# Values as the weights of their product, agents streamed twice, and more load buffers in an agent-attention and cosine-FFN kernel

## The chip, the cores and the metric

The kernel runs on one core of a Trainium2 chip. The metric is the device time in microseconds of one execution; lower is better. Inputs lie in device memory in the layouts that the kernel asks for (q and k transposed, v in tiles of 120 rows, the weights as 64-bit patterns), and the output is written transposed.

The core has five engines that matter here. PE multiplies matrices: it loads up to 128 columns of weights (recorded as LDWEIGHTS, row PEld), then streams the other operand past them (MATMUL, row PE) and writes to PSUM, an accumulator memory of eight banks with 512 float32 columns each. DVE and ACT work element by element and read PSUM. POOL works on SBUF, the main on-chip memory. SP issues the DMA transfers between device memory and SBUF, in order.

## The reference

Cut to what matters, with B = 4 batches, N = 12480 tokens each, C = 128 channels, 49 agents and a hidden width of 2048:

```python
def sm(a, b):                              # softmax over b's rows of a @ b.T / sqrt(128)
    s = scale * (a @ b.transpose(0, 2, 1)); s = s - s.max(-1, keepdims=True)
    e = np.exp(s)
    return e / (e.sum(-1, keepdims=True) + 1e-09)
agent_v = sm(agents, k) @ v                # 49 x 128 per batch
attn    = sm(q, agents) @ agent_v          # N x 128 per batch
h       = attn.reshape(B * N, 128) @ w_in  # 49920 x 2048
out     = (h * np.cos(h)) @ w_out          # 49920 x 128
```

The tokens of k and v meet only in `agent_v`. A batch's tokens of q cannot pass through the second half before its `agent_v` is there.

## The kernel before, in words

**Tiles.** A batch's 12480 tokens are 13 groups (`NG`) of 960 (`GRP`); a group is 8 tiles (`GT`) of 120 tokens (`TT`). A load of a group of q, k or v is 480 KB.

**One batch's agents** (class `Agents`, with `Fast` on top of it). `scores` (L144) loads a group of k into one of three `xt` buffers and makes eight products with 120 columns of k as the weights and the 49 agents streaming (helper `scores`, L81, the product at L87). They land in one PSUM bank; ACT copies them to `s` (L153), and DVE keeps a running maximum (L157). `top`, `across` and `spread` reduce the maximum over the tiles and partitions and lay it out over all partitions. `shift` subtracts it (DVE or POOL, L182), `exp` takes the exponential on ACT, `add` sums them on POOL. `values` (L195) loads a group of v into one of three `vt` buffers and makes eight products with the exponentials of a tile (120 x 49) as the weights and v (120 x 128) streaming (L200). The result, 49 x 128, is added by DVE to `o` (L204). `total` and `turn` follow: `turn` (L213) multiplies `o` by `fold`, a 49 x 113 matrix made of two identities. That transposes `o` and puts it side by side twice, in columns 0 to 48 and 64 to 112, as `av` (L219). It also forms the inverse of the sums. `project` multiplies `av` with `w_in`, so the hidden layer of batch b is then one product of 113 rows per token.

**The weights.** `w_in` and `w_out` arrive as float64 and are turned into float32 on DVE by eight bit operations for each chunk of 512 columns (L103 to L111). The raw chunk stands in a `vt` buffer, as the groups of v do. `product` forms w_in times w_out, for which the transposes are at L129 and the products at L133.

**The steps.** From the 832 steps (L469) comes the output. Each takes 480 tokens and 256 hidden columns: two products into a two-bank PSUM tile `ph` (L476; three such tiles), the cosine on ACT (L479, into one of three `c` buffers), (cos - 1) times h on DVE (L481), and four steps later two products into the output (L497). There are 208 steps per batch.

**What sets the order.** Before the steps, batch 0's agents, the weights and the first three groups of q are worked off alone, in the order of a list, `pre`: `pre(n, f, ...)` puts f at place n, and the places are run one after the other. Key scores of group g stand at place g, a chunk of `w_in` at 3c + 1, the first queries at 14, 15 and 16, shift, exponential and values of group k at 15 + k, 16 + k and 17 + k, a chunk of `w_out` at 16 + 3c and its product a place later, `turn` at 30. During the steps, a second list, `plan`, puts the agents of batches 1 to 3 and the queries of all groups between steps; `extra` gives each piece with products a step of its own. The framework may still move an engine's instructions past their neighbours when it lays out the queues (the exponentials of the steps and the load of the sine table are held in place with `keep_in_program_order`). On the chip the engines take their instructions from their queues in order; SP likewise, and a load waits there until its buffer is free.

**PSUM.** Six banks are the three `ph` tiles, two banks are the small tiles `one`. The key scores, the values, the queries and the transposes before the change all take `one`.

The lower part of the program, from L519, is a slower path for inputs out of range; it isn't run with these inputs.

Of the kernel before, what the change touches and what calls it, by code (L numbers as in the profile page):

```python
# [40 lines left out]
def agent_attention_cos_ffn(ctx, tc, qT, kT, v, agT, w_in, w_out, outT):  # L41
# [17 lines left out]

    ident = const.tile([P, P], F32, name="ident")  # L60
    make_identity(nc, ident)

    fold = const.tile([NA, KR], F32, name="fold")
    nc.gpsimd.memset(fold, 0.0)
    for part in (fold[:, :NA], fold[:, HI:]):
        nc.gpsimd.affine_select(out=part, in_=part, compare_op=ALU.not_equal, fill=1.0,
                                base=0, pattern=[[-1, NA]], channel_multiplier=1)
    ones = const.tile([P, 1], F32, name="ones")
    nc.gpsimd.memset(ones, 1.0)
    half_pi = const.tile([P, 1], F32, name="half_pi")  # L70
# [7 lines left out]

    fits = const.tile([KR, NB], F32, name="fits")

    def scores(sb, src, b, ps):  # L81

        xt = sb.tile([P, GRP], F32, name="xt", bufs=3)
        nc.sync.dma_start(xt, src)
        ps = ps[:TT, :GT * NA].rearrange("p (t a) -> p t a", a=NA)
        for t in range(GT):
            nc.tensor.matmul(ps[:, t, :], xt[:, t * TT:(t + 1) * TT], ag[:, b, :], start=True, stop=True)  # L87
        return ps

    class Weights:  # L90


        def __init__(self, sb, psum, tag, bufs):
            self.sb, self.psum = sb, psum
            self.scratch = dict(name=tag, bufs=bufs)

        def single(self, src, out):

            raw = self.sb.tile([P, 512, 2], U32, name="vt", bufs=3)
            nc.sync.dma_start(raw, src)  # L100
            lo, hi = raw[:, :, 0], raw[:, :, 1]
            ex, sign, man = (self.sb.tile([P, 512], U32, **self.scratch) for _ in range(3))
            nc.vector.tensor_scalar(ex, hi, 20, 0x7FF, op0=ALU.logical_shift_right, op1=ALU.bitwise_and)  # L103
            nc.vector.tensor_scalar(sign, hi, 0x80000000, None, op0=ALU.bitwise_and)
            nc.vector.tensor_scalar(ex, ex, 1151.0, 896.0, op0=ALU.min, op1=ALU.max)
            nc.vector.tensor_scalar(man, hi, 0xFFFFF, 0x100000, op0=ALU.bitwise_and, op1=ALU.bitwise_or)
            nc.vector.tensor_scalar(ex, ex, 896.0, None, op0=ALU.subtract)
            f = man.bitcast(F32)
            nc.vector.scalar_tensor_tensor(f, lo, 2.0 ** -32, man, op0=ALU.mult, op1=ALU.add)
            nc.vector.scalar_tensor_tensor(ex, ex, 23, sign, op0=ALU.logical_shift_left, op1=ALU.bitwise_or)  # L110
            nc.vector.scalar_tensor_tensor(out, f, 2.0 ** -20, ex.bitcast(F32), op0=ALU.mult, op1=ALU.mult)  # L111
# [25 lines left out]
    class Agents:  # L137

        def __init__(self, sb, psum, b, alone=False):
            self.sb, self.psum, self.b, self.alone = sb, psum, b, alone

        def scores(self, g):  # L144
            sb = self.sb
            if g == 0:
                self.s = sb.tile([TT, NT, NA], F32, name="s", bufs=1)
                self.run = sb.tile([TT, GT, NA], F32, name="run", bufs=1)
                self.o = sb.tile([NA, P], F32, name="o", bufs=2)
                self.es = sb.tile([TT, GT, NA], F32, name="es", bufs=1)  # L150
            ps = scores(sb, kT[self.b, :, g * GRP:(g + 1) * GRP], self.b, self.psum())
            s = self.part(g)
            nc.scalar.copy(s, ps)  # L153
            if g == 0:
                nc.vector.tensor_copy(self.run, s)
            else:
                nc.vector.tensor_max(self.run, self.run, s)  # L157

        def part(self, g, n=1):
            return self.s[:, g * GT:(g + n) * GT, :]  # L160
# [32 lines left out]
                nc.gpsimd.tensor_add(self.es, self.es, self.part(g))  # L193

        def values(self, g):  # L195
            vt = self.sb.tile([TT, GT, P], F32, name="vt", bufs=3)
            nc.sync.dma_start(vt, v[self.b, :, g * GT:(g + 1) * GT, :])
            e, po = self.part(g), self.psum()[:NA, :P]
            for t in range(GT):
                nc.tensor.matmul(po, e[:, t, :], vt[:, t, :], start=(t == 0), stop=(t == GT - 1))  # L200
            if g == 0:
                nc.vector.tensor_copy(self.o, po)
            else:
                nc.vector.tensor_add(self.o, self.o, po)  # L204

        def total(self):

# [2 lines left out]
            nc.vector.tensor_reduce(self.es2[:, :NA], self.es.rearrange("p t a -> p a t"), axis=AX.X, op=ALU.add)  # L210
            nc.vector.tensor_copy(self.es2[:, HI:], self.es2[:, :NA])

        def turn(self):  # L213

            pa = self.psum()
            nc.tensor.matmul(pa[:, :KR], self.o, fold, start=True, stop=True)
            nc.tensor.matmul(pa[:KR, 256:257], self.es2, ones[:TT], start=True, stop=True)
            self.av = self.sb.tile([P, KR], F32, name="av", bufs=1)
            nc.vector.tensor_copy(self.av, pa[:, :KR])  # L219
            z = self.sb.tile([KR, 1], F32, name="z", bufs=1)  # L220
            nc.vector.tensor_scalar_add(z, pa[:KR, 256:257], EPS)
            self.rz = self.sb.tile([KR, 1], F32, name="rz", bufs=1)
            nc.vector.reciprocal(self.rz, z)

# [2 lines left out]
    class Fast(Agents):  # L227

        def project(self, c, a):

            cs = slice(c * 512, (c + 1) * 512)
            pw = self.psum()
            nc.tensor.matmul(pw[:KR], self.av, win[:, cs], start=True, stop=True)  # L233
            if c == 0:
                self.big = self.sb.tile([KR, DFF // 512], F32, name="big", bufs=1)
            nc.scalar.activation(a[:, cs], pw[:KR], AF.Copy, scale=self.rz)
            x = a[:, cs].bitcast(F32)
            nc.vector.tensor_reduce(self.big[:, c:c + 1], x, axis=AX.X, op=ALU.max, apply_absolute_value=True)

            on = nc.vector if self.alone else nc.gpsimd  # L240
            on.tensor_scalar(a[:, cs], x, FAST_MAX, -FAST_MAX, op0=ALU.min, op1=ALU.max)

        def project_out(self, wio, b1, b2):
# [25 lines left out]
    with ExitStack() as pools:  # L269
# [76 lines left out]
            t = sb.tile([1, 1], F32, name="sine", bufs=1)  # L346
            tc.keep_in_program_order(nc.scalar.activation(t, half_pi[:1], AF.Sin))

        ab = [Fast(sb, small, b, b == 0) for b in range(NB)]
        if NG == 13:  # L350
            pieces0 = [(0, 1, 2), (3, 4, 5, 6, 7), (8, 9, 10, 11, 12)]
            pieces1 = [(0, 1, 2, 3), (4, 5, 6, 7), (8, 9, 10, 11, 12)]
# [6 lines left out]
        for g in range(NG):  # L359
            pre(g, ab[0].scores, g)  # L360
        for c in range(NF // 4):
            pre(3 * c + 1, ws.w_in, c)
        pre(NG, ab[0].top)
        pre(NG, ab[0].across)
        pre(NG, ab[0].spread)
        for i, n in enumerate(pieces[0][0]):
            pre(NG + 1 + i, query, n, pieces[0][0])
        for j, (g, n) in enumerate(lots):
            for k in range(g, g + n):
                pre(NG + 2 + k, ab[0].shift, k, 1, nc.gpsimd if k % 3 == 2 else nc.vector)  # L370
# [13 lines left out]
            ws.product(c, w_parts.pop(c), po_w[0], wio)  # L384

        for c in range(NF // 4):
            pre(NG + 3 + 3 * c, w_out_of, c)
            pre(NG + 4 + 3 * c, w_product, c)
        pre(end - 2, query_exp, pieces[0][0])
        pre(end - 1, query_sums, pieces[0][0])  # L390
        pre(end - 1, query_weights, 0)
        pre(end, sine_table)
        pre(end, query_turned, 0)
        pre(end, ab[0].total)
        pre(end, ab[0].turn)
        for c in range(DFF // 512):
            pre(end + 1, ab[0].project, c, a[0])
        pre(end + 1, ab[0].project_out, wio, b1[0], b2[0])
# [36 lines left out]
        for b in range(1, NB):  # L435
# [20 lines left out]
                plan(t, ab[b].add, g)  # L456
                t = extra(t, ab[b].values, g) + 1
            plan(t, ab[b].total)
            t = extra(t + 1, ab[b].turn) + 1
            i = b % 2  # L460
            for c in range(DFF // 512):
                t = extra(t, ab[b].project, c, a[i]) + 1
# [56 lines left out]
    with tc.If(far):  # L519
        with ExitStack() as pools:  # L520
# [72 lines left out]
                nc.sync.dma_start(dst, osb)  # L593

            for b in range(NB):
                ab = Agents(sb, small, b, True)
                for g in range(NG):
                    ab.scores(g)
                ab.top()
# [5 lines left out]
                    ab.add(g)  # L605
                    ab.values(g)
                ab.total()
                ab.turn()
                for c in range(DFF // 512):
                    cs = slice(c * 512, (c + 1) * 512)  # L610
                    pw = small()
# [32 lines left out]
```

## Time and profile before

| | |
|---|---|
| Median of 3 runs | 1332.18 us (1330.01 to 1332.27) |
| Profiled execution | 1332.36 us, span 1330.6 us |
| Before the steps | about 121 us of the span |
| PE, DVE, ACT, POOL busy | 1231.0, 1094.5, 1010.4, 331.2 us |
| Mean granted clock of PE | 0.978 |
| Moved by DMA | 107.74 MB |

A row of the profile names the line, the engine, the operation, the tile written and the tiles read, the shapes and the count, then the busy time in us with the mean of one in ns, then the idle time ahead of them and what ended it. A float32 product is recorded as two LDWEIGHTS and two MATMUL records; where the products of the steps read float32r, there is one of each. Matmuls are pipelined, so the mean of one is longer than the distance between two.

### The profile page before, as it was taken

To read this page: it belongs to the slowest core of one execution; us is meant where nothing else is said; L and a number is where in the kernel's file an instruction comes from. 1 tells how busy PE (TensorE), PEld (TensorE's weight loads), DVE (VectorE), ACT (ScalarE), POOL (GpSimd) and SP (SyncE) were. 2 spreads that over 40 slices of the span, in tenths; PEclk is the share of its full clock that TensorE was granted. 3 is DMA by queue.
4 is the path that set the end of the run, shared out by engine and by line. 5 is a ranking of instruction groups with operands and counts; after the bars stand their busy time and mean duration, and the time that the engine had idled before them with its cause. 6 is when DMAs were issued, how large, how long until landed. Compare 5 with 4: busy or idle time off the path is not lost.

```text
span 1330.6 us, 17227 instructions
## 1 busy us (share of the span) xinstructions
PE 1231.0 (93%) x6357; PEld 971.9 (73%) x6357; DVE 1094.5 (82%) x1221; ACT 1010.4 (76%) x1115; POOL 331.2 (25%) x357
## 2 busy tenths in 40 slices
PE   8878999999799999996999999996999999999997
PEld 8866778777587788775876688775786666666664
DVE  3566878878778988887789988887779999999997
ACT  1124778866768987667689988767679999999997
POOL 1231211331512122315122211514113222122220
PEclk9979989999899999998999999998999999999999
DMA  6665234233242132332420033230420000000000
GB/s 209 172 163 134 90 102 122 89 92 105 72 119 75 59 105 89 120 107 74 117 60 30 30 104 123 72 105 30 119 75 16 30 30 30 30 15 31 30 30 33
DMA packets 31017, 107.74 MB, mean 81 GB/s; under 512 B 3436, under 2 KB 3820, under 8 KB 30924
## 3 DMA queue, kind: packets, MB, share of 16 engines
q1 hardware_dynamic: 30924, 106.54, 26.6%
q8 instruction: 53, 0.87, 0.3%
q14 instruction: 40, 0.33, 0.1%
HBM read 80.97 MB, written 25.56 MB: 80 GB/s over the span
## 4 chain that ended last, share of the span: by engine, by line
PE 67%; DVE 13%; ACT 11%; issue 5%; POOL 2%; DMA 1%; ACTq 0%; SPq 0%; POOLq 0%
PE ph L476 23%; PE one L497 16%; PE one L87 14%; DVE r L481 10%; PE one L200 7%; ACT c L479 5%; ACT osb L499 3%; PE one L492 2%; PE one L333 2%; PE one L493 1%; DVE mx L304 1%; ACT e L314 1%; POOL es L193 1%; PE one L233 1%; ACT p L335 1%
## 5 line engine op out<-in xcount | busy, mean ns | idle before, releaser
L481 DVE SCALAR_TENSOR_TENSOR r<-c,ph 128x960 fp32r<-128x960 f32 x832 | 926.2, 1149 | 119.9 <-ACT c L479 109.6
L479 ACT ACTIVATE c<-ph,half_pi 128x960 f32<-128x960 f32 x832 | 864.4, 1066 | 208.4 <-PE ph L476 191.3
L476 PE MATMUL ph<-pT,a 113*128 113x480 f32 x1664 | 540.1, 406 | 24.2 <-DVE r L481 20.8
L497 PE MATMUL one<-r,w 128*128 128x480 f32 x1664 | 516.1, 390 | 0.7 <-DVE r L481 0.7
L476 PEld LDWEIGHTS ph<-pT,a 113*128 113x128 f32 x1664 | 287.3, 191 | 150.9 <-DVE r L481 88.3
L497 PEld LDWEIGHTS one<-r,w 128*128 128x128 f32 x1664 | 309.2, 190 | 52.0 <-issue 7.6
L87 PEld LDWEIGHTS one<-ag,xt 128*120 128x120 f32 x1664 | 216.9, 206 | 25.3 <-ACT osb L499 10.8
L324 POOL TENSOR_TENSOR p<-e,rz 120x392 f32<-120x392 f32 x52 | 43.9, 846 | 758.6 <-PE one L333 716.8
L87 PE MATMUL one<-ag,xt 128*120 128x49 f32 x1664 | 215.6, 285 | 8.7 <-DMA xt<-kT 5.0
L200 PE MATMUL one<-vt,s 120*49 120x128 f32 x832 | 112.7, 294 | 37.0 <-ACT osb L499 26.7
L200 PEld LDWEIGHTS one<-vt,s 120*49 120x49 f32 x832 | 97.9, 134 | 53.6 <-ACT osb L499 27.9
L339 POOL TENSOR_TENSOR pT<-p,pT 49x480 fp32r<-49x480 f32 x104 | 126.6, 1217 | 8.0
L338 POOL CAST pT<-p 49x480 fp32r<-49x480 f32 x104 | 60.8, 585 | 59.1 <-ACT p L335 54.1
L153 ACT COPY s<-one 120x392 f32<-120x392 f32 x52 | 25.2, 485 | 45.0 <-PE one L87 44.8
L499 ACT COPY osb<-one 128x480 f32<-128x480 f32 x104 | 57.8, 555 | 2.1 <-PE one L497 2.1
L304 DVE TENSOR_REDUCE mx<-one 120x8 f32<-120x392 f32 x52 | 29.3, 564 | 35.3 <-PE one L87 35.2
L492 PE MATMUL one<-pT,b 113*128 113x480 f32 x104 | 46.3, 445 | 11.7 <-ACT osb L499 6.7
L182 POOL TENSOR_TENSOR s<-s,mxb 120x1568 f32<-120x1568 f32 (+2 forms) x13 | 35.8, 2778 | 72.8 <-DVE mxb L178 72.8
L193 POOL TENSOR_TENSOR es<-es,s 120x392 f32<-120x392 f32 x48 | 50.0, 1042 | 13.1 <-ACT s L186 9.4
L492 PEld LDWEIGHTS one<-pT,b 113*128 113x128 f32 x104 | 19.7, 189 | 34.3 <-issue 12.5
L157 DVE TENSOR_TENSOR run<-run,s 120x392 f32<-120x392 f32 x48 | 27.0, 562 | 18.8 <-ACT s L153 18.8
L333 PE MATMUL one<-ident,p 120*113 120x120 f32 x208 | 37.9, 283 | 4.4 <-ACT s L153 1.8
(84 smaller groups left out, 405.1 us busy)
## 6 DMA issues: line engine op xcount, KB each, us to landing
xt<-kT SPq DMA_DIRECT2D x52, 480.0 KB, 3.5
xt<-qT SPq DMA_DIRECT2D x52, 480.0 KB, 3.5
vt<-v SPq DMA_DIRECT2D x52, 480.0 KB, 4.3
outT<-osb SPq DMA_DIRECT2D x51, 480.0 KB, 2.5
vt<-w_in SPq DMA_DIRECT2D x4, 512.0 KB, 4.7
vt<-w_out SPq DMA_DIRECT2D x4, 512.0 KB, 5.2
outT<-osb SPq DMA_DIRECT2D x2, 240.0 KB, 2.0
ag<-agT SPq DMA_DIRECT2D x1, 98.0 KB, 2.1
```

Source lines behind the costliest of these rows:

```text
L87: nc.tensor.matmul(ps[:, t, :], xt[:, t * TT:(t + 1) * TT], ag[:, b, :], start=True, stop=True)
L193: nc.gpsimd.tensor_add(self.es, self.es, self.part(g))
L200: nc.tensor.matmul(po, e[:, t, :], vt[:, t, :], start=(t == 0), stop=(t == GT - 1))
L333: nc.tensor.transpose(pt[:KR, t * TT:(t + 1) * TT], p_in[n % 2][:, t, :KR], ident[:TT, :TT])
L338: nc.gpsimd.tensor_copy(pT[own, c], p[own])
L339: nc.gpsimd.tensor_sub(pT[other, c], p[own], pT[own, c].bitcast(F32))
L476: nc.tensor.matmul(ph[:, j, :CH], ai[:, f], pTs[q % 3][:, c], start=True, stop=True)
L479: nc.scalar.activation(cos, h, AF.Sin, bias=half_pi, scale=1.0)
L481: nc.vector.scalar_tensor_tensor(r, cos, 1.0, h, op0=ALU.subtract, op1=ALU.mult)
L492: nc.tensor.matmul(po, b1[k], pTs[q % 3][:, c], start=True, stop=False)
L497: nc.tensor.matmul(po, w1[:, f, :], r[:, j, :], start=False, stop=(f == NF - 1))
L499: nc.scalar.copy(osb[:, c * CH:(c + 1) * CH], po)
```

## The change

The operands of the values' product change places: a tile of v (120 x 128) is now the weights, and the 49 exponentials stream, twice over, through an access pattern with a step of zero (`twice`). The result is 128 x (2 x 49). It is written to columns 0 to 48 and 64 to 112 of a bank (`copies`), which is the layout of `av`. So `o`, `fold` and the fold product go, and `turn` becomes `inverse`, with only the product for the sums.

Batch 0 gets `wide`, a function that hands out the steps' two-bank tiles `ph`. Its key scores stream the agents twice as well: four tiles of 98 columns in each of the two banks, of which ACT reads the first 49 of each 98. Its values accumulate over all 13 groups in one bank of one such tile, and DVE copies them out once at the end. In batches 1 to 3 each group's values still go to a small tile, and DVE adds them to `av`.

Batch 0's odd groups of k are loaded into the steps' `c` buffers, the even ones into `xt`. The raw chunks of the weights get two buffers of their own (`raw`), and `vt` has four. In the list `pre`, chunks of `w_in` move from 3c + 1 to 3c + 2, chunks of `w_out` and their products one place later, and the first three queries from 14, 15, 16 to 14, 18, 22.

```diff
-    fold = const.tile([NA, KR], F32, name="fold")
...
+    def twice(x):
+        return x.unsqueeze(1).to_broadcast([x.shape[0], 2, NA])
...
+    def scores_twice(xt, src, b, ps):
+        nc.sync.dma_start(xt, src)
+        ps = ps[:TT, :, :HT * 2 * NA].rearrange("p h (t x a) -> p h t x a", x=2, a=NA)
+        for t in range(GT):
+            nc.tensor.matmul(ps[:, t // HT, t % HT], xt[:, t * TT:(t + 1) * TT], twice(ag[:, b, :]),
+                             start=True, stop=True)
+        return ps[:, :, :, 0, :]
...
-            raw = self.sb.tile([P, 512, 2], U32, name="vt", bufs=3)
+            raw = self.sb.tile([P, 512, 2], U32, name="raw", bufs=2)
...
-                self.o = sb.tile([NA, P], F32, name="o", bufs=2)
+                av = sb.tile([P, 2 * HI], F32, name="av", bufs=2)
+                self.av, self.sums = av[:, :KR], self.copies(av)
+                nc.gpsimd.memset(av[:, NA:HI], 0.0)
...
-            ps = scores(sb, kT[self.b, :, g * GRP:(g + 1) * GRP], self.b, self.psum())
+            src = kT[self.b, :, g * GRP:(g + 1) * GRP]
             s = self.part(g)
-            nc.scalar.copy(s, ps)
+            if self.wide is None:
+                nc.scalar.copy(s, scores(sb, src, self.b, self.psum()))
+            else:
+                if g % 2:
+                    xt = sb.tile([P, 2, CH], F32, name="c", bufs=3).rearrange("p j x -> p (j x)")
+                else:
+                    xt = sb.tile([P, GRP], F32, name="xt", bufs=3)
+                ps = scores_twice(xt, src, self.b, self.wide())
+                nc.scalar.copy(s.rearrange("p (h t) a -> p h t a", h=2), ps)
...
+        def copies(self, x):
+            return x[:, :2 * HI].rearrange("p (x a) -> p x a", x=2)[:, :, :NA]
...
-            vt = self.sb.tile([TT, GT, P], F32, name="vt", bufs=3)
+            vt = self.sb.tile([TT, GT, P], F32, name="vt", bufs=4)
             nc.sync.dma_start(vt, v[self.b, :, g * GT:(g + 1) * GT, :])
-            e, po = self.part(g), self.psum()[:NA, :P]
+            lone = self.wide is not None
+            if g == 0 or not lone:
+                self.po = self.copies(self.wide()[:, 0] if lone else self.psum())
+            e, po = self.part(g), self.po
             for t in range(GT):
-                nc.tensor.matmul(po, e[:, t, :], vt[:, t, :], start=(t == 0), stop=(t == GT - 1))
-            if g == 0:
-                nc.vector.tensor_copy(self.o, po)
-            else:
-                nc.vector.tensor_add(self.o, self.o, po)
+                nc.tensor.matmul(po, vt[:, t, :], twice(e[:, t, :]), start=(t == 0 and (g == 0 or not lone)),
+                                 stop=(t == GT - 1 and (g == NG - 1 or not lone)))
+            if g == (NG - 1 if lone else 0):
+                nc.vector.tensor_copy(self.sums, po)
+            elif not lone:
+                nc.vector.tensor_add(self.sums, self.sums, po)
...
-        def turn(self):
+        def inverse(self):
             pa = self.psum()
-            nc.tensor.matmul(pa[:, :KR], self.o, fold, start=True, stop=True)
-            nc.tensor.matmul(pa[:KR, 256:257], self.es2, ones[:TT], start=True, stop=True)
-            self.av = self.sb.tile([P, KR], F32, name="av", bufs=1)
-            nc.vector.tensor_copy(self.av, pa[:, :KR])
+            nc.tensor.matmul(pa[:KR, :1], self.es2, ones[:TT], start=True, stop=True)
...
-        ab = [Fast(sb, small, b, b == 0) for b in range(NB)]
+        def pair():
+            return ps_h.tile([P, 2, 512], F32, name="ph")
+        ab = [Fast(sb, small, b, None if b else pair) for b in range(NB)]
...
-            pre(3 * c + 1, ws.w_in, c)
+            pre(3 * c + 2, ws.w_in, c)
...
-            pre(NG + 1 + i, query, n, pieces[0][0])
+            pre(NG + 1 + 4 * i, query, n, pieces[0][0])
...
-            pre(NG + 3 + 3 * c, w_out_of, c)
-            pre(NG + 4 + 3 * c, w_product, c)
+            pre(NG + 4 + 3 * c, w_out_of, c)
+            pre(NG + 5 + 3 * c, w_product, c)
```

More of the change, by code (lines that the diff above doesn't have):

```diff
@@ L61, in agent_attention_cos_ffn @@
     make_identity(nc, ident)
-    fold = const.tile([NA, KR], F32, name="fold")
[L64 to L67, printed above, removed]
     ones = const.tile([P, 1], F32, name="ones")
@@ L137, in agent_attention_cos_ffn, with __init__ @@
     class Agents:
-        def __init__(self, sb, psum, b, alone=False):
-            self.sb, self.psum, self.b, self.alone = sb, psum, b, alone
+        def __init__(self, sb, psum, b, wide=None):
+            self.sb, self.psum, self.b, self.wide = sb, psum, b, wide
         def scores(self, g):
@@ L211, in total @@
             nc.vector.tensor_copy(self.es2[:, HI:], self.es2[:, :NA])
-        def turn(self):
+        def inverse(self):
             pa = self.psum()
-            nc.tensor.matmul(pa[:, :KR], self.o, fold, start=True, stop=True)
-            nc.tensor.matmul(pa[:KR, 256:257], self.es2, ones[:TT], start=True, stop=True)
-            self.av = self.sb.tile([P, KR], F32, name="av", bufs=1)
-            nc.vector.tensor_copy(self.av, pa[:, :KR])
+            nc.tensor.matmul(pa[:KR, :1], self.es2, ones[:TT], start=True, stop=True)
             z = self.sb.tile([KR, 1], F32, name="z", bufs=1)
-            nc.vector.tensor_scalar_add(z, pa[:KR, 256:257], EPS)
+            nc.vector.tensor_scalar_add(z, pa[:KR, :1], EPS)
             self.rz = self.sb.tile([KR, 1], F32, name="rz", bufs=1)
@@ L238, in project @@
             nc.vector.tensor_reduce(self.big[:, c:c + 1], x, axis=AX.X, op=ALU.max, apply_absolute_value=True)
-            on = nc.vector if self.alone else nc.gpsimd
+            on = nc.vector if self.wide else nc.gpsimd
             on.tensor_scalar(a[:, cs], x, FAST_MAX, -FAST_MAX, op0=ALU.min, op1=ALU.max)
@@ L394, in agent_attention_cos_ffn @@
         pre(end, ab[0].total)
-        pre(end, ab[0].turn)
+        pre(end, ab[0].inverse)
         for c in range(DFF // 512):
@@ L458, in agent_attention_cos_ffn @@
             plan(t, ab[b].total)
-            t = extra(t + 1, ab[b].turn) + 1
+            t = extra(t + 1, ab[b].inverse) + 1
             i = b % 2
@@ L595, in agent_attention_cos_ffn @@
             for b in range(NB):
-                ab = Agents(sb, small, b, True)
+                ab = Agents(sb, small, b)
                 for g in range(NG):
@@ L607, in agent_attention_cos_ffn @@
                 ab.total()
-                ab.turn()
+                ab.inverse()
                 for c in range(DFF // 512):
```

## The prediction

> **What bounds the kernel now.** I read the page first, then the busy times by stage.
>
> ```profile
> span 1330.6 us, 17227 instructions
> L87 PEld LDWEIGHTS one<-ag,xt 128*120 128x120 f32 x1664 | 216.9, 206 | 25.3 <-ACT osb L499 10.8
> L87 PE MATMUL one<-ag,xt 128*120 128x49 f32 x1664 | 215.6, 285 | 8.7 <-DMA xt<-kT 5.0
> L200 PE MATMUL one<-vt,s 120*49 120x128 f32 x832 | 112.7, 294 | 37.0 <-ACT osb L499 26.7
> L200 PEld LDWEIGHTS one<-vt,s 120*49 120x49 f32 x832 | 97.9, 134 | 53.6 <-ACT osb L499 27.9
> ```
>
> ```profile
> 4.97:46.80 41.83, 41.81 (x208) 41.65 (x208) 20.38 (x44) 5.82 (x12) 0.48 (x2) 1.00 0.66 208
> 50.60:112.60 62.00, 49.04 (x306) 43.84 (x305) 34.70 (x66) 13.40 (x24) 19.87 (x19) 0.89 0.63 165
> 121.50:1200.00 1078.50, 1011.98 (x5326) 798.44 (x5325) 912.93 (x984) 866.32 (x944) 277.87 (x288) 0.98 0.25 77
> 1200.00:1330.60 130.60, 118.69 (x477) 82.10 (x477) 118.54 (x111) 117.50 (x126) 24.20 (x27) 0.99 0.07 28
> ```
>
> The columns of the second fence are the stage, its length, then busy time of PE, PEld, DVE, ACT and POOL, the clock, the DMA share and GB/s. A float32 product leaves two records: values are 52 groups of 8 products, and L200 has 832. From 121.5 us on the steps run, PE-bound while batches overlap them and ACT/DVE-bound at the end. The first 121.5 us serve batch 0 alone: 13 groups of key scores (4.97 to 46.80), then queries, values and the weight product (50.60 to 112.60). The chain of waits shows their pace (start, length, what):
>
> ```profile
> 1.20 3.64 DMA xt<-kT
> 4.97 41.83 PE one L87 x208
> 50.61 6.58 PE one L87 x32
> 61.76 3.31 PE one L200 x16
> ...
> 87.45 4.27 DMA vt<-v
> 91.85 3.54 PE one L200 x16
> ...
> 100.86 4.96 DMA vt<-v
> ...
> 106.99 1.09 PE ph L133 x8
> 108.08 4.50 PE one L200 x40
> ...
> 113.18 0.40 PE one L216 x2
> ...
> 113.90 0.28 DVE av L219
> ```
>
> ```profile
> 329.91 1.17 PE one L87 x11
> ```
>
> A score record takes 41.83/208 = 0.201 us in the first stage and 1.17/11 = 0.106 us later (last row, from the steps). A values record takes 3.31/16 = 0.207 us at 61.76 and 4.50/40 = 0.112 us at 108.08. The same instructions run at two speeds a factor of two apart: the first stage runs at half the TensorE clock. (The clock column says 1.00 there, but nothing before 64.65 us agrees with that.) The clock follows what streams. These are consecutive windows, with PE's busy time, its records and the clock:
>
> ```profile
> 74.89:78.30 3.41, 3.41 (x17) 0.50 0.48 97
> 78.30:81.71 3.41, 1.07 (x8) 1.00 0.20 34
> 81.71:85.13 3.42, 2.51 (x11) 0.50 0.89 267
> 85.13:88.54 3.41, 3.41 (x18) 0.50 0.10 13
> 88.54:91.95 3.41, 1.33 (x12) 1.00 0.73 196
> ```
>
> It is wholly 0.50 or wholly 1.00 in each, so it is decided every 3.41 us. At half clock a values record streams 128 columns in two passes, 256 columns in 0.213 us (3.41/16), so a window has room for about 4096. The windows at 74.89 and 85.13, nearly full of such records, were followed by full clock; that at 81.71, with 11 records (11 x 256 = 2816, 69%), was not. Score records stream 2 x 49 = 98 columns in 0.201 us, 17 per window, 1666 columns (41%): 41.83 us of them never raised the clock. At full clock, 1.07 us of work at 78.30 was too little to keep it. The limit lies above 69% and below a full window.
>
> **The change, part by part.**
>
> *Key scores of batch 0.* The weights stay 120 columns, the agents stream twice: 196 columns per record. A record now lasts 0.201 us because of its load of 2 x 120 = 240 columns (PEld is busy 41.65 of 41.83 us); 196 fit beneath, so even at half clock it costs nothing more. But the window then holds 17 x 196 = 3332 columns, 81%. I take it that this is over the limit. PE starts at 4.97; the first whole window ends 3.4 to 6.8 us later, say 5.1 us and 25 records; the other 183 go at 0.106 us, 19.4 us. Sum 24.5 instead of 41.83: **-17.3 us**. Transfers, SP or DVE could bind instead (two windows, then SP's longest waits from 0 to 122 us: total, times, longest):
>
> ```profile
> 4.00:8.00 4.00, 3.03 (x16) 3.06 (x16) 0.39 (x2) 0.00 (x0) 1.45 (x4) 1.00 0.99 389
> 71.47:74.89 3.42, 0.30 (x4) 0.31 (x4) 3.42 (x5) 2.49 (x4) 3.26 (x3) 1.00 1.01 287
> ```
>
> ```profile
> SPq L84 <- PE one L87: 51.9, 16, 8.2
> SPq L197 <- PE one L200: 33.1, 11, 7.5
> SPq L197 <- DVE r L109: 9.3, 3, 8.2
> ```
>
> Saturated transfers move 287 (values and w_out) to 389 GB/s (keys). The stage loads 13 x 480 + 4 x 512 KB = 8.49 MB: 21.8 to 29.6 us from 1.2 us on, so done at 23 to 31, against PE's 29.5. SP now waits on PE for a free xt (51.9 us in all); six buffers instead of three, the spare ones the steps' cosine tiles, let it run five groups ahead, and those tiles are free long before step 0 writes them. DVE has 20.4 us of work here, from about 8 us on (first w_in chunk): done near 28.4, so w_in, one place later, stays covered. At worst the last transfer at 31 and a group's products after it, near 32: -15. If the clock stays low: 0.
>
> *The gap.* From 46.80 to 50.61 the maximum goes through DVE and three small products; that stays, PE idles 3.8 us, and the clock falls again.
>
> *Values of batch 0.* 128 weight columns of v, 2 x 49 = 98 moving, instead of 49 and 128. The load is 2 x 128 = 256 columns, as many as streamed before, so the record stays at 0.213 or 0.112 us. Weights and stream of 128 each stand in the trace (L133, 8 in 1.09 us, 0.136 with the tail of the last), which bounds it above; below, only the stream counts, 98/128 x 0.112 = 0.086. I take 0.112, because a load of 120 columns already runs at 0.106. But a window of them at half clock now holds 196/256 = 77%, not 100%.
>
> The Trainium skill speaks against this part ("TensorE: Matmul & The Clock Gate", LDWEIGHTS): a load takes the columns divided by 1.2 GHz, 107 ns for 128, so two passes would be an estimated 213 ns a record even at full clock, some 60 us more over the 624 records of the later batches. The 0.106 us of L87 with 120 columns, which that rule puts at 200 ns, contradicts it here, so I leave it no chance.
>
> The stage now: query 0 cold 16 x 0.201 = 3.2 us, values 0 3.4 us (shift and exponential of group 0 hide under query 0), query 1 3.2 us: 9.8 us. Queries are spread by four places, so values 0 no longer waits for three of them. Then values and products follow on; a product's records stream 100%, and a window half of each holds 88%, so I expect full clock about 1.5 windows later: 5.1 us, 24 records. Of 208 + 32 + 16 + 48 = 304 records 232 are left, 24.8 us. Sum 39.7.
>
> The 62 us of before held 13 us of idle PE: the chain's waits for v, because SP could not issue (its waits on PE L200, and on DVE L109 where the weight chunks shared vt). Now vt has four buffers of its own, the chunks two, and w_out starts a place later. Loads are 13 x 480 + 3 x 480 + 4 x 512 KB = 9.96 MB, at 287 GB/s 34.7 us, some of it prefetched. DVE had 34.70 us; 13 additions are gone:
>
> ```profile
> L204 DVE TENSOR_TENSOR o<-o,one 49x128 f32<-49x128 f32 x48 | 13.1, 273 | 18.0 <-PE one L200 18.0
> ```
>
> That is 3.5 us, so 31 us are left. Both are near the 39.7, so I add 5 us of stalls, somewhat under half of the 13: 45 instead of 62, **-17 us** (-24 without stalls and with an early rise; 0 if the clock stays low: 48 x 0.201 + 240 x 0.213 + transposes = 63 us). The 13 groups accumulate in one two-bank tile, a second holds the weight product, so one of three is left until the steps; their step 1 waits for the copy of the sums, which the projections need first anyway.
>
> *Turn to inverse.* The fold product (0.40) and its copy (0.28) go, the copy of the sums (about the 0.27 of L204) comes: **-0.4 us**.
>
> *Batches 1 to 3.* 39 groups, 624 records, at 0.112 us as before: **0**, with bounds (0.086 - 0.112) x 624 = -16 and (0.136 - 0.112) x 624 = +15. PE is what bounds there, nothing hides it. The additions stay on DVE, a little narrower, beside PE; three fold products (1.2 us) go. After the exponentials of a batch the clock starts low, and values raise it more slowly: up to 1.7 us at three places.
>
> Sum against the profiled execution, 1332.36 (span 1330.6; median 1332.18): 1332.4 - 17.3 - 17 - 0.4 = 1297.7, **1298 us**.
>
> **The rivals.**
> *B, the values stay cold.* 77% is just over a limit known only to lie above 69%, and any stall takes a window below it. Then the stage takes 63 us and only the scores gain: 1332.4 - 17.3 - 0.4 = 1315. For: before, the clock fell in it three times. Against: the products fill windows.
>
> *C, nothing warms.* The limit is above 81%. Scores keep 0.201, the values stage is 63 + some stalls for 62: about 1334, no change. For: nothing between 69% and a full window was seen. Against: 81% is nearer the top, and the window at 74.89 was not quite full.
>
> *D, slower: the strided output.* A values product now writes two runs of 49 columns 64 apart. Nothing in the trace does that with a matmul. If each column then took two turns, a record would take 2 x 196 columns at 256 per 0.112 us, 0.172 us: 60 ns more, on 832 records 50 us, so 1298 + 50 = 1348. It decides from 35/832 = 42 ns a record on. For: PE bounds the steps. Against: the score outputs, 49 words each and side by side, start at an odd word every second time and still run at the load's 0.106.
> A page of the Trainium skill says as much as D ("PSUM — Partial Sum Buffer", Specifications): any non-contiguous access pattern slows matmuls significantly. No run here shows it yet.
>
> *E, better.* The clock rises in the first window and DVE and loads leave no stalls: 45 becomes 38 and the scores 23: about 1289.
>
> **How the numbers follow.** Forecast with E: 0.63 (its own range 1286 to 1309); B 0.20; C 0.09; D 0.08. The range 1285 to 1321 holds the forecast and B and leaves out C and D. A difference of 0.2% (2.7 us) is about what can be told from none. Faster: forecast, B and a little of C, 0.84. Same: half of C, 0.04. Slower: D and the rest of C, 0.12.
>
> **What would show it.** The scores' 208 records in 24 to 26 us (41.8 means C), the last at 0.105; values records at 0.21 until a product has run, then near 0.11 (0.21 to the end: B; 0.17: D, and the same from 346 us on); first step near 85 us instead of 121; the steps' length unchanged within 5 us. The forecast is wrong if the stage after the scores takes DVE or SP as its chain and not PE, or if the steps lengthen.

## The result and the profile after

The changed kernel takes 1290.75 us (median of 4, 1290.17 to 1291.06) against 1332.15 us (median of 4): a ratio of 0.9692, 95% interval 0.9676 to 0.9709. The forecast was 1298, with a range from 1285 to 1321 that holds the time. The sum behind it is less right than its total, which owes its nearness to errors that partly cancel. First the span of the changed kernel and its two groups of value products, from the list that keeps shapes apart:

```profile
span 1288.7 us, 17186 instructions
L224 PE MATMUL ph<-s,vt 120*128 120x98 f32 x208 | 30.7, 313 | 0.0
L224 PE MATMUL one<-s,vt 120*128 120x98 f32 x624 | 81.3, 285 | 26.6 <-ACT osb L524 26.6
```

Busy times in three stretches, with the prediction's columns: 5 us of batch 0's scores, 5 us of its values, and the whole stage of the values.

```profile
20.00:25.00 5.00, 5.00 (x50) 5.00 (x49) 4.86 (x12) 1.46 (x3) 0.00 (x0) 1.00 0.97 356
55.00:60.00 5.00, 5.00 (x49) 5.00 (x48) 0.00 (x0) 1.52 (x3) 2.79 (x4) 1.00 0.89 248
36.30:85.05 48.75, 44.18 (x311) 43.71 (x310) 34.55 (x56) 13.76 (x25) 26.81 (x25) 0.80 0.78 208
```

The chain of waits of the changed kernel, up to the first steps:

```profile
5.25 13.43 PE ph L93 x96
18.67 0.02 issue
18.70 0.49 ACT s L171
...
33.18 0.49 DVE run L175
33.69 0.82 DVE m L185
...
36.31 4.16 PE one L85 x20
40.47 3.50 PE ph L224 x16
...
56.38 1.76 PE ph L224 x16
...
60.02 0.57 DVE mx L326
...
63.66 1.17 DVE r L110
64.83 1.16 DVE r L111
65.99 1.15 DVE r L112
67.14 0.34 DVE r L113
...
80.80 4.23 PE ph L224 x26
...
85.06 0.27 DVE av L227
...
88.03 0.43 DVE a L263
...
92.80 0.06 DVE fits L276
```

Two places in the chain of the kernel before that the prediction did not show:

```profile
116.89 1.40 DVE a L241
...
122.59 0.06 DVE fits L254
```

With these the 41.9 us between the two spans can be laid out. The marks are the first query behind the maximum (50.61 and 36.31), the last value (112.6 and 85.06) and `fits` (122.59 and 92.80), which ends batch 0's own work.

| Stage | Before | After | Difference | Predicted |
|---|---|---|---|---|
| Start, key scores, maximum | 50.6 | 36.3 | -14.3 | -17.3 |
| First queries, values, weight product | 62.0 | 48.75 | -13.2 | -17 |
| Sums to the last projection | 10.0 | 7.7 | -2.3 | -0.4 |
| The remaining steps | 1208.0 | 1195.9 | -12.1 | 0 |

A score record takes 0.105 us in the middle of its stage, where groups of 16 records start 1.68 us apart (the 50 records of the window at 20 include those that only reach into it), and 13.43/96 = 0.140 on the mean of the first 13 us, a part of them at half clock. A values record takes 3.50/16 = 0.219 us at 40.47 and 1.76/16 = 0.110 us at 56.38. So both products cost per record what was forecast, also where the result is two runs of 49 columns. The last line of the table was not foreseen: the steps have as many value records as before, and they became 12.1 us shorter.

**Where the steps gained.** Nearly all of it lies where the values of batches 1 to 3 stand between the steps. The weight loads at one such place in the kernel before (start, length, line, what; in brackets PEld's idle time ahead of it):

```profile
372.75 0.32 PEld L476 LDWEIGHTS ph<-pT,a 113*128 113x128 f32 x2
373.41 1.70 PEld L200 LDWEIGHTS one<-vt,s 120*49 120x49 f32 x16 [0.34 <-issue]
375.29 0.30 PEld L497 LDWEIGHTS one<-r,w 128*128 128x128 f32 x2 [0.18 <-issue]
```

and at the same place in the changed kernel:

```profile
341.63 0.32 PEld L501 LDWEIGHTS ph<-pT,a 113*128 113x128 f32 x2
341.99 1.97 PEld L224 LDWEIGHTS one<-s,vt 120*128 120x128 f32 x16
343.88 0.30 PEld L522 LDWEIGHTS one<-r,w 128*128 128x128 f32 x2
```

In the steps a weight load starts while the product before it still streams. Before, the first load of 49 columns did not: PEld stood for 0.34 us, and for 0.18 us on the way back to 128 columns. After, both waits are gone. From the first load of the step's two products to the first of the next two it was 375.29 - 372.75 = 2.54 us and is now 343.88 - 341.63 = 2.25: 0.29 us less per group, over 39 groups 11.3 of the 12.1 us. The groups of loads add it up, before and after, with all that ended their idle time:

```profile
L200 PEld LDWEIGHTS one<-vt,s 120*49 120x49 f32 x832 | 97.9, 134 | 53.6 <-ACT osb L499 27.9 <-issue 11.5 <-DVE r L110 4.9
```

```profile
L224 PEld LDWEIGHTS one<-s,vt 120*128 120x128 f32 x624 | 81.5, 205 | 30.4 <-ACT osb L524 27.9 <-DVE av L229 0.2
```

"issue", a wait for nothing that the profile shows, was 11.5 us and is no longer there. That the width of the loads is the cause, and not the shorter stream or the additions, is settled by two runs below.

### The profile page after: what moved, and what is told of

It reads as the page before. It is cut to its first block, busy times and chain, and to the rows that moved or that the text cites. A ratio compares the mean times of both kernels' runs of the same rounds, so it can differ in the third digit from the quotient of the medians.

```text
span 1288.7 us, 17186 instructions
## 1 busy us (share of the span) xinstructions
PE 1195.5 (93%) x6349; PEld 961.0 (75%) x6349; DVE 1091.2 (85%) x1205; ACT 1009.6 (78%) x1115; POOL 333.7 (26%) x358
## 4 chain that ended last, share of the span: by engine, by line
PE 66%; DVE 15%; ACT 12%; issue 5%; POOL 1%; DMA 0%; ACTq 0%; SPq 0%; POOLq 0%; DVEq 0%
PE ph L501 24%; PE one L522 16%; PE one L85 11%; DVE r L506 10%; PE one L224 6%; ACT c L504 6%; ACT osb L524 3%; PE one L517 3%; PE one L355 2%; PE one L518 1%; PE ph L224 1%; DVE mx L326 1%; ACT e L336 1%; PE ph L93 1%; ACT p L357 1%
## 5 line engine op out<-in xcount | busy, mean ns | idle before, releaser
L85 PEld LDWEIGHTS one<-ag,xt 128*120 128x120 f32 x1456 | 173.6, 187 | 19.3 <-ACT osb L524 11.0
L85 PE MATMUL one<-ag,xt 128*120 128x49 f32 x1456 | 172.4, 267 | 2.6 <-ACT osb L524 1.7
L224 PE MATMUL one<-s,vt 120*128 120x98 f32 x624 | 81.3, 285 | 26.6 <-ACT osb L524 26.6
L224 PEld LDWEIGHTS one<-s,vt 120*128 120x128 f32 x624 | 81.5, 205 | 30.4 <-ACT osb L524 27.9
L517 PE MATMUL one<-pT,b 113*128 113x480 f32 x104 | 46.1, 443 | 12.0 <-ACT osb L524 6.7
L355 PEld LDWEIGHTS one<-ident,p 120*113 120x113 f32 x208 | 28.9, 179 | 17.3 <-ACT osb L524 12.1
L518 PE MATMUL one<-pT,b 113*128 113x480 f32 x104 | 39.6, 381 | 0.0
```

The costliest lines, as they stand in the source:

```text
L224: nc.tensor.matmul(po, vt[:, t, :], twice(e[:, t, :]), start=(t == 0 and (g == 0 or not lone)), stop=(t == GT - 1 and (g == NG - 1 or not ...
L355: nc.tensor.transpose(pt[:KR, t * TT:(t + 1) * TT], p_in[n % 2][:, t, :KR], ident[:TT, :TT])
L517: nc.tensor.matmul(po, b1[k], pTs[q % 3][:, c], start=True, stop=False)
L518: nc.tensor.matmul(po, b2[k], pTs[q % 3][:, c], start=False, stop=False)
```

## The experiments

Times are medians; ratios stand against the kernel before, run beside it on the same chip, with 95% intervals. Dots in an edit stand for lines not shown. "The theory" is at first that of the prediction: the clock for batch 0's scores, SP's waits for the buffers.

**Agents streamed once in the scores.**

```diff
-            nc.tensor.matmul(ps[:, t // HT, t % HT], xt[:, t * TT:(t + 1) * TT], twice(ag[:, b, :]),
+            nc.tensor.matmul(ps[:, t // HT, t % HT], xt[:, t * TT:(t + 1) * TT], ag[:, b, :],
...
-        return ps[:, :, :, 0, :]
+        return ps
```

> The changed kernel, but batch 0's key scores stream the agents once (49 columns); tiles, buffers and places as changed. Theory clock: the second stream raises the clock, so the 208 score records go back from about 26 us to 41.8 us at 0.201 us each, and the time rises by 11 to 16 us to about 1304 (what DVE no longer holds up is kept). Rival buffers: the scores gained because six buffers and two-bank tiles keep PE fed; then the records keep 0.105 us and the time stays at 1291 within 2 us.

1301.4 us, ratio 0.9770 (0.9753 to 0.9786), 10.7 us above the changed kernel. Its chain:

```profile
5.04 38.62 PE ph L93 x192
```

A record takes 38.62/192 = 0.201 us again, with all the buffers in place. The clock did it. The rise is just below the band: the first query comes 15.0 us later (51.26 against 36.31), but the values stage is 3.2 us shorter than in the changed kernel and the steps 1.7, which was not followed up.

**The swap alone.** What is left of the change are the operands of the values and `inverse`; the diff is against the changed kernel.

```diff
-            raw = self.sb.tile([P, 512, 2], U32, name="raw", bufs=2)
+            raw = self.sb.tile([P, 512, 2], U32, name="vt", bufs=3)
...
-            vt = self.sb.tile([TT, GT, P], F32, name="vt", bufs=4)
+            vt = self.sb.tile([TT, GT, P], F32, name="vt", bufs=3)
...
-        ab = [Fast(sb, small, b, None if b else pair) for b in range(NB)]
+        ab = [Fast(sb, small, b) for b in range(NB)]
...
-            pre(3 * c + 2, ws.w_in, c)
+            pre(3 * c + 1, ws.w_in, c)
...
-            pre(NG + 1 + 4 * i, query, n, pieces[0][0])
+            pre(NG + 1 + i, query, n, pieces[0][0])
...
-            pre(NG + 4 + 3 * c, w_out_of, c)
-            pre(NG + 5 + 3 * c, w_product, c)
+            pre(NG + 3 + 3 * c, w_out_of, c)
+            pre(NG + 4 + 3 * c, w_product, c)
```

> The kernel before with the swapped operands of the values' product alone, in all batches (and with it no fold product): old scores, buffers and places, values of batch 0 added by DVE group by group. Theory switch: 128 weight columns in place of 49 let the load run under the product before it, so each of the 39 groups in the steps is 0.29 us shorter: 11 to 12 us less in the steps, and the first stage about as before (within 4 us): 1320. Rival: the 12 us that the steps lost come from something else in the change (buffers, phase of the clock windows); then the time is 1330 to 1334.

1322.0 us, ratio 0.9919 (0.9903 to 0.9936): 10.9 us less. `fits` stands at

```profile
126.25 0.07 DVE fits L276
```

so batch 0 is 3.7 us slower (122.59 before), and the steps after it take 1320.0 - 126.25 = 1193.8 us, 14.2 less than before. The swap alone gives the steps their gain (2 us more of it than in the changed kernel, which was not followed up), and in batch 0 alone it costs 3.7 us.

**The weights' width, with nothing else changed.** Here v streams 128 columns as before; only the batches 1 to 3 load more columns of the exponentials, the second time 65 in place of 64 (`s` gets one more tile of zeros, so that the last load has columns to read).

```diff
...
-            e, po = self.part(g), self.psum()[:NA, :P]
+            e, wide = self.s.rearrange("p t a -> p (t a)"), 64 if self.b else NA
+            po = self.psum()
...
-                nc.tensor.matmul(po, e[:, t, :], vt[:, t, :], start=(t == 0), stop=(t == GT - 1))
+                at = (g * GT + t) * NA
+                nc.tensor.matmul(po[:wide, :P], e[:, at:at + wide], vt[:, t, :], start=(t == 0), stop=(t == GT - 1))
+            po = po[:NA, :P]
```

> The kernel before, with the weights of the values' product of batches 1 to 3 widened from 49 to 64 columns of the exponentials (the further rows of the result are not read); v streams 128 columns as before. Theory switch, with a border between 64 and 65 columns of weights: no load of 64 columns starts under a product of 128, as with 49, so the time stays at 1332 within 2 us. Theory switch without such a border (any difference in width counts): also 1332. Rival stream (the later batches gained because 98 columns stream instead of 128): 1332.

> The same with 65 columns of weights. Theory switch with a border between 64 and 65: the load now starts under the product before it, each of 39 groups is 0.25 to 0.29 us shorter, 10 to 11 us less: 1321 to 1323, although 128 columns still stream and DVE still adds 128 columns. Any-difference theory and rival stream: 1332 within 2 us.

64 columns: 1333.4 us, ratio 1.0009 (0.9998 to 1.0020). 65 columns: 1320.7 us, ratio 0.9917 (0.9887 to 0.9947). The groups of these loads, with 64 columns and with 65:

```profile
L203 PEld LDWEIGHTS one<-vt,s 120*64 120x64 f32 x624 | 71.7, 144 | 41.4 <-ACT osb L503 27.9 <-issue 11.0 <-DVE o L208 1.9
```

```profile
L203 PEld LDWEIGHTS one<-vt,s 120*65 120x65 f32 x624 | 74.7, 145 | 33.8 <-ACT osb L503 27.9 <-DVE o L208 1.9 <-DVE o L206 0.2
```

One more column takes 12.7 us off: the 11.0 us of "issue" are there at 64 and gone at 65. Neither the shorter stream nor DVE's narrower addition plays a part, as both are unchanged here. The Trainium skill says that loads are pulled ahead of products in flight where the row groups don't conflict or the load goes to the background weights ("TensorE: Matmul & The Clock Gate", Part 2, LDWEIGHTS); it does not name the number of columns as a condition, and these two runs do.

**The old buffers.**

```diff
-            raw = self.sb.tile([P, 512, 2], U32, name="raw", bufs=2)
+            raw = self.sb.tile([P, 512, 2], U32, name="vt", bufs=3)
...
-                if g % 2:
-                    xt = sb.tile([P, 2, CH], F32, name="c", bufs=3).rearrange("p j x -> p (j x)")
-                else:
-                    xt = sb.tile([P, GRP], F32, name="xt", bufs=3)
+                xt = sb.tile([P, GRP], F32, name="xt", bufs=3)
...
-            vt = self.sb.tile([TT, GT, P], F32, name="vt", bufs=4)
+            vt = self.sb.tile([TT, GT, P], F32, name="vt", bufs=3)
```

> The changed kernel with the old buffers: three for v and the raw weight chunks together, three for k. Theory: SP stands behind the weight chunks again, so the values stage of batch 0 grows by 3 to 10 us, the scores by 1 to 3 us, the steps stay: 1295 to 1303. Rival: with the clock up, the first stage is bound by DVE and PE and not by loads; then it stays at 1291 within 2 us.

1306.3 us, ratio 0.9809 (0.9792 to 0.9825), 15.6 above the changed kernel and above the band. In the chain of its profiled execution (1302.8 us, the shortest of the four) the loads come back:

```profile
12.67 5.28 DMA xt<-kT
...
20.01 5.43 DMA xt<-kT
...
85.95 4.54 DMA vt<-v
```

With the clock up, three buffers of k no longer last: they cover 3 x 16 x 0.201 = 9.6 us of products at the low clock but 3 x 16 x 0.105 = 5.0 us at the high one, and a load is issued only when a buffer is free. But that is the smaller part. In this execution the first query comes 3.9 us later than in the changed kernel (40.17), the values stage takes 58.5 us, 9.8 more, and the steps take 2.0 less. So most of the loss lies in the values stage, where v and the chunks share three buffers again. The buffers of k and those of v and the chunks were not tried apart.

**The old places.**

```diff
-            pre(3 * c + 2, ws.w_in, c)
+            pre(3 * c + 1, ws.w_in, c)
...
-            pre(NG + 1 + 4 * i, query, n, pieces[0][0])
+            pre(NG + 1 + i, query, n, pieces[0][0])
...
-            pre(NG + 4 + 3 * c, w_out_of, c)
-            pre(NG + 5 + 3 * c, w_product, c)
+            pre(NG + 3 + 3 * c, w_out_of, c)
+            pre(NG + 4 + 3 * c, w_product, c)
```

> The changed kernel with the old places of the weight chunks and of the first queries in the list. Theory: three queries of 49 streamed columns stand before values 0, but PE does the same work, so it is worth 2 us either way: 1289 to 1294. Rival: the weight chunks, one place earlier, free DVE sooner in the values stage, where DVE set the end from 60 to 79 us; then 2 to 5 us less, 1286 to 1289.

1294.1 us, ratio 0.9706 (0.9690 to 0.9722). The interval overlaps that of the changed kernel (0.9676 to 0.9709), so the new places are worth little and perhaps nothing. The rival, by which the old places would be the faster ones, is out.

**How near the limit of the clock is.** Instead of the agents twice, the first 86 or 92 columns of the agents of two batches stream.

```diff
-            nc.tensor.matmul(ps[:, t // HT, t % HT], xt[:, t * TT:(t + 1) * TT], twice(ag[:, b, :]),
+            nc.tensor.matmul(ps[:, t // HT, t % HT], xt[:, t * TT:(t + 1) * TT],
+                             ag.rearrange("p b a -> p (b a)")[:, b * NA:b * NA + 86],
...
-        return ps[:, :, :, 0, :]
+        return ps[:, :, :, :NA]
```

> The changed kernel; batch 0's scores stream 86 columns (49 agents and 37 of the next batch's, which are not read) instead of 98: 2 x 86 x 17 = 71.7% of a window at half clock. With the limit at about three quarters, as the windows of the trace put it (72.3% and 76.0% did not raise the clock, 71.3% and 75.2% did), the clock stays low over all 208 records: 41.8 us for the scores, some 1302. If the limit lies below 71%: as with 98, 1291.

> The same with 92 columns, 76.7% of a window, the share that a window of values has in the changed kernel. Limit at about three quarters: the clock rises in the first whole window, 1291. Limit above 77%: it stays low over the scores, 1302, and values alone could never raise it.

With 86 columns 1301.8 us, with 92 columns 1286.7 us (one run each). The chains, first 86, then 92:

```profile
5.09 41.89 PE ph L93 x208
```

```profile
5.23 22.92 PE ph L93 x192
```

All 208 records with 86 columns take 0.201 us; with 92 the clock rises. A record lasts as long as its load of 120 columns, so with 86, 92 and 98 columns PE streams for 86/120 = 71.7%, 76.7% and 81.7% of a window at half clock. So for these even scores the limit lies between 71.7% and 76.7%, and 98 columns have only 5 to 10 points to spare. It is no sharp rule for every window: the expectation for 86 columns counts windows of mixed work at 72.3% and 76.0% that did not raise the clock, and others at 71.3% and 75.2% that did. That 92 columns came out 4 us below 98, in a single run, is not explained.

**Values that stream 128 columns.** Seven of eight products of batch 0 stream two runs of 64.

```diff
...
+                if lone and t < GT - 1:
+                    nc.tensor.matmul(self.full, vt[:, t, :], flat[:, at:at + HI].unsqueeze(1).to_broadcast([TT, 2, HI]),
+                                     start=(t == 0 and g == 0), stop=False)
+                    continue
...
```

> The changed kernel, with batch 0's values streaming 128 columns (two runs of 64, of which the last 15 belong to the next tile and are not read) in seven of eight products. At half clock a window of them then holds 97% instead of 77%. Theory clock: the clock rises 3 to 7 us sooner than at 52.8 us and does not hang at the limit; the values stage is 2 to 5 us shorter: 1286 to 1289. Rival: DVE sets the end of that stage whatever PE does; 1291 within 1.5 us.

1289.5 us, ratio 0.9692 (0.9669 to 0.9714): no difference from the changed kernel that can be told, above the theory's band and at the edge of the rival's. The time ran out elsewhere. DVE stood idle for 7.67 us up to 63.47, waiting for POOL's sums of the exponentials, which stand ahead of a chunk of w_out in its queue here; the chunk itself, issued at 57.73 behind three loads of v, landed only 5.9 us later. Then PE worked 0.81 of the 5 us from 65 on, while DVE worked all of them, for the most part on that chunk.

```profile
65.00:70.00 5.00, 0.81 (x4) 0.84 (x5) 5.00 (x12) 0.62 (x1) 0.39 (x1) 0.70 0.20 52
```

**Clock and chunks, apart and together.** From here on the theory was that the values stage has two binders one behind the other. On top of the 128 columns the first kernel keeps PE going in the gap, streams the first queries twice, and moves the weight chunks. The second has all of that but the chunks, the third is the changed kernel with the chunks alone moved.

```diff
...
+        def keep_on(n):
+            if not early:
+                early.append(pair())
+            for _ in range(n):
+                nc.tensor.matmul(early[0][:TT, 0, :P], ab[0].last[:, :TT], ident, start=True, stop=True)
...
+        pre(NG - 1, keep_on, 12)
...
+            if piece[0] == 0:
+                ps = scores_twice(sb.tile([P, GRP], F32, name="xt", bufs=3), src, b, early[0])
...
-            pre(3 * c + 2, ws.w_in, c)
+            pre((2, 5, 8, NG + 1)[c], ws.w_in, c)
...
-            pre(NG + 4 + 3 * c, w_out_of, c)
-            pre(NG + 5 + 3 * c, w_product, c)
+            pre(NG + 3 + 2 * c, w_out_of, c)
+            pre(NG + 5 + 2 * c, w_product, c)
```

> The same as the kernel with 128 streamed columns, and in addition: twelve products whose result is not read behind batch 0's key scores, so that PE is not idle while the maximum is formed; the first three queries stream the agents twice; the last chunk of w_in is converted after the maximum and the chunks of w_out stand two places apart instead of three. Theory clock: it stays up through the gap, and queries and values run at 0.105 and 0.112 us from 34 us on: 6 to 12 us less than the changed kernel, 1279 to 1285. Rival: DVE and the loads bind the stage; 1287 to 1291.

> The kernel that was kept on (unread products in the gap, queries and values of batch 0 streaming more), but the weight chunks at the places of the changed kernel. Theory clock: the clock made its gain, so most of the 9 us stay: 1282 to 1286. Rival places: the gain came from the chunks of w_in and w_out, on which DVE and SP hang; then 1288 to 1291.

> The changed kernel with only the weight chunks moved (the last of w_in after the maximum, those of w_out two places apart). Theory clock: PE stays at half clock from 33 to about 52 us, so little is gained: 1288 to 1292. Rival places: 1281 to 1285. If both are needed: this one 1286 to 1288 and the other about the same.

Everything together: 1281.4 us, ratio 0.9630 (0.9607 to 0.9653), faster than both given kernels. All but the chunks: 1287.9, ratio 0.9675 (0.9656 to 0.9695). Chunks only: 1285.6, ratio 0.9658 (0.9641 to 0.9674). The last two medians fall between the bands of their expectations and in none of them. `fits` in the three, in this order:

```profile
84.33 0.07 DVE fits L286
```

```profile
91.71 0.06 DVE fits L286
```

```profile
87.32 0.06 DVE fits L276
```

Against 92.80 the chunks alone bring 5.5 us, the rest alone 1.1, both 8.5 (in the medians 5.1, 2.9 and 9.4). The theory of the clock as the one that mattered in this stage falls: alone it brings little, and where DVE has the chunks early it brings 8.5 - 5.5 = 3.0 us. So there are at least two binders. A third one stands in the kernel with all but the chunks, whose chain goes through POOL's sums:

```profile
55.25 2.21 POOL es L215
...
62.95 0.83 DVE es L245
```

DVE waits 6.37 us for them, with a chunk behind them in its queue that was issued at 49.62 and landed within 7.3 us. What the clock alone would bring without this wait is not shown. In the kernel with both, the scores are bound by PE to the end (24.83 us for 208 records, 0.119 each), where the changed kernel's chain leaves PE after 96 records:

```profile
5.58 24.83 PE ph L93 x208
```

## Why the prediction was right or wrong

**Key scores: right in cause, 3 us too much.** A record takes 0.105 us instead of 0.201, as the step said; streaming once and 86 columns take the gain away, 98 and 92 bring it. PE had its 208 records done in 25.2 us, at 30.4, within the 24 to 26 foreseen, although the clock rose only 6.6 us after the first of them. The term of the sum that was off is the end of the stage. I let PE set it and put DVE's end at 28.4 us, a little ahead. The chain leaves PE at 18.67 and stays on DVE, with its maxima and the conversion of w_in, until 33.69. DVE has as much to do there as before, and it was filled to 4.86 of 5 us while PE, now twice as fast, gave it a group every 1.7 us. The stage's cover for the conversions was the slowness that the change took away.

**Values of batch 0: the right direction, 4 us too much, and the wrong binder named.** I let the clock rise 14.9 us after the maximum (9.8 + 5.1), and it took 52.78 - 36.31 = 16.5 (windows with PE's busy time, records and clock):

```profile
45.95:49.36 3.41, 3.41 (x17) 0.50 0.88 247
49.36:52.78 3.42, 3.42 (x18) 0.50 0.48 134
52.78:56.19 3.41, 3.41 (x32) 1.00 0.22 42
```

That is nearly right, and rival B fell: the clock did not stay low to the end, though the window at 45.95, with queries and values in it, went by without raising it. The mis-sized term is the 5 us of stalls. From 60.02 to 79.31 the chain is DVE's, in the main on the last two chunks of w_out. Behind it come the last product and the values at 80.80, which run at 4.23/26 = 0.163 because PE had been kept waiting and the clock had fallen once more (0.66 on the mean from 80 to 85). So the sign of being wrong that the prediction named, DVE as the chain of this stage, came true for 19.3 of its 48.75 us, and the first step, which was to come near 85, has its DVE work at 91.7 (121.5 before).

DVE had done nothing from 55 to 60 us. Next in its queue stood the third query's maximum, for which PE formed the scores only by 59.99, and the next chunk was not there either. SP's queue shows why (start, length, line, what):

```profile
49.81 4.92 SPq L218 DMA_DIRECT2D vt<-v  x2
54.78 0.39 SPq L107 DMA_DIRECT2D raw<-w_out  x1
```

The chunk's load stands behind two loads of v that wait for their buffers. It landed 6.0 us after its issue, and DVE came to it at 63.66, behind the query's operations and the shifts. Then DVE was slow: the first three operations on the chunk took 1.15 to 1.17 us in the chain, the fourth 0.34. POOL was adding from 59.55 to 66.86, and the long operations on the last chunk fall into POOL's work as well. The kernel before shows the same: from 75.20 on, with POOL at work until 79.52, these operations take 1.15 to 1.16 us. Over the two chunks the extra lengths add up to some 6 us, an estimate from the chain's long and short pieces, as much as the 5 us of stalls. No run takes POOL's work away, so that POOL slows DVE here is read from the timing alone.

I had seen that DVE's 31 us and PE's 39.7 were near each other, and treated DVE's work as if it could be spread evenly over the stage.

**Turn to inverse: 0.4 foreseen, 2.3 measured.** The step counted the fold product and the copies alone. The clamp behind the first projection took 1.40 us before and 0.43 after, which is 1.0 of it. Before, POOL was at work during it (115.54 to 118.01), after, it was not; no run tried that apart.

**Batches 1 to 3: 0 foreseen, -12.1 measured.** The step that failed is "the record stays at 0.213 or 0.112 us" as the whole price. It does stay (0.110), but the price of a group is also its two ends, where a load of 49 columns was not started under a product of 128. The row that tells it was there to see: of the 53.6 us of idle time ahead of L200's loads, which the prediction quotes, 11.5 are "issue" in the list of groups. The prediction gives no account of them. The lower bound, -16, held the result for another reason than the one that it was worked out from, the stream: that was luck. The steps' length was to stay within 5 us, and it did not. What the step said of the clock came in part: behind the exponentials it stays low for 13.65 us instead of 10.24 in two of the three batches.

**The rule on the length of loads**, which the prediction gave no chance, is not borne out: 128 columns of weights go at 0.110 us a record.

**Rival C** (nothing warms) fell with the first stage. **Rival D** (strided output) fell too: two runs of 49 columns go at 1.76/16 = 0.110 us, the 128 columns in one run in the kernel with both at 0.114 (14 in 1.59 us in its chain). The Trainium skill's page that says that any non-contiguous access slows matmuls ("PSUM — Partial Sum Buffer", Specifications) is not borne out by this pattern of 49 words per run. But the load of 2 x 128 columns covers the stream of 2 x 98, so a slowing of less than 256/196, some 30%, would not show here.

```profile
70.09 1.59 PE ph L231 x14
```

**The total.** 1297.7 + 3.0 + 3.8 - 1.9 - 12.1 = 1290.5: two terms were 6.8 us too large, and two others, of which one was not counted at all, 14.0 too small. The total is 7.2 us off where the errors of its parts add up to 20.8: that they partly cancel is luck.

## What to carry to other kernels

Look at the two ends of a block of products and not only at its pace: if the weights before it and in it differ in width across 64 columns, as 49 or 64 next to 128 did here, each change can cost a wait that shows as idle PEld under "issue", and widening the narrow weights costs nothing where the load lies beneath the stream. Where short streams keep PE at half clock, streaming more columns than are needed can be free, because the load is the longer of the two; count streamed columns in the window. A stage that gets twice as fast uses up its buffers in half the time, and the next binder should be sought in the order of the queues, not in the totals.

## What was not expected of the hardware

Loads of 49 and of 64 columns between products with 128 columns of weights were not started under them (with 49 columns 0.34 us of idle PEld going in and 0.18 coming back); loads of 65 were. The clock follows streamed columns, not loads: with the load busy in every moment of a window, 71.7% left it at half in 208 records, and 76.7% raised it, in one run each. And the clock's own column cannot be read where the profiler has no record: in the kernel before the first record of the clock is at 64.65 us, and the column says 1.00 for the 41.83 us of scores that ran at half speed.
